# A convolution stem with its gradients on one core: Gelu in plain steps with its sums on ScalarE, three leaves by three products, stored sums of x, a shorter last product

## The chip, the cores and the metric

The kernel runs on one core of one Trainium2 chip. Its time is device microseconds of one execution, and the median of several executions stands for a kernel. All arrays are bf16, and products are added up in fp32 in PSUM. TensorE (PE) multiplies; VectorE (DVE) and ScalarE (ACT) work element by element; SyncE (SP) issues nearly all DMAs. "us" is microseconds.

## The reference

A one-dimensional convolution with 31 taps and stride 2 over B = 2 sequences of T = 16000 positions with D = 256 channels gives L = 7985 positions. Each channel of each sequence is then normalised over its positions, scaled and shifted, and passed through Gelu in its tanh form. The kernel also returns the gradients of x, w, gamma and beta for a given gradient of the output.

```python
h = jnp.einsum('blc,cd->bld', x[:, 0:s * L:s, :], w[0])
for i in range(1, K):
    h = h + jnp.einsum('blc,cd->bld', x[:, i:i + s * L:s, :], w[i])
mu = jnp.einsum('bld->bd', h)[:, None, :] / L
var = jnp.einsum('bld->bd', (h - mu) ** 2)[:, None, :] / L
h = (h - mu) / jnp.sqrt(var + 1e-5)
h = h * gn_gamma[None, None, :] + gn_beta[None, None, :]
return _gelu(h)
```

The outputs are Gelu's result and, from the vector-Jacobian product with grad_out, dx, dw, dgamma and dbeta.

## The kernel before

**Order.** The program first records every operation with `add`: its engine, what it reads and writes, and a function that issues it. Then `emit` issues the operations in the order that the table STEPS gives, as differences of positions in the record. Each engine works off its own instructions in that order and waits where operands are late. The order is thus written out by hand; the costs beside each `add` do not set it. SP's queue holds loads, stores and DMA transposes alike.

**Forward convolution (0 to about 385 us).** For each sequence b there are four chunks c of 2048 output positions (three full, one of 1841). A chunk is computed in three branches B_, A, C_, and a branch in three leaves B_, A, C_, since a convolution in two parts can be had from three products instead of four: the sums of inputs are made on DVE (`f_sums`, L492), the differences of weights too (`w_sub`, L473). A leaf is computed in one of two ways. `f_leaf` runs over all its taps: 64 matmuls of 256 columns. By three products it is split once more: `f_three_b` multiplies a difference of weights (WD) into one half of a PSUM buffer with 16 matmuls, ACT copies that half negated into the other (L550), and `f_three_ac` adds 32 more. A branch that is `split` does this for all three leaves; a `plain` one only for leaf B_. The set FV lists the branches that are split: nearly all of b = 0; for b = 1 the branches B_ and, in chunk 3, A and C_. The differences WD live in bytes that the Gelu of b = 0 uses later, so `f_again` computes four of them anew ahead of chunk 3 of b = 1. The evictions are at L574 (`keep`) and L596 on ACT, and the joins of leaves at L623 on DVE.

**Gelu.** Sequence 0's normalisation, Gelu and its derivative run during the forward convolution of sequence 1 (about 205 to 375 us), sequence 1's during the input gradient of sequence 0 (about 410 to 575 us): 8 units of 2048 elements per partition each, `gelu_unit`. A unit's steps: two ACT passes per half for y and its square (L860), a scalar_tensor_tensor on DVE (L862), sigmoid and another pass on ACT (L864, L866), a tensor_scalar (L868) and products on DVE (L872), and per half one accumulating copy on ACT (L885) and one tensor_tensor_reduce on DVE (L888) for the two sums that gamma and beta need. The units take turns with two sets of tiles (GT); for b = 0 set 1 lies at REG + 20480 and up. Two DMA transposes (L309) turn y of each unit for the output.

**Input gradient (about 390 to 803 us).** Stages G0 to G7, one per chunk and sequence, with matmuls of 512 columns at L1068.

**Weight gradient (803 to 1095 us).** Nine combinations n of a sum or difference of x with one of the gradient, stages W0 to W8, each with up to three products over both sequences. `x_tile` fetches the four tiles of x for the next combination: a raw block, a sum of two raw blocks (`x_raw` twice and `w_add`, L1322), or, for sequence 0, a stored sum that `x_pre` made during the forward convolution (xs_d). A combination begins with two adds into XSUM (L1322), sums of neighbouring rows (`pair_x`) and differences of the gradient (`leaf_d`, both L1312), and `pair_d` (L1418). PE's matmuls are at L1359 (`w_pairs`, `w_single`). The results are gathered by `w_done` (sums at L1365, the last one at L1387).

## Time and profile before

| | before |
|---|---|
| median of 3 runs | 1096.27 us (1095.95 to 1098.23) |
| the profiled execution, its own time | 1097.28 us |
| its span in the profile | 1095.2 us |
| PE busy, matmuls | 1080.6 us, 8123 recorded |
| PE weight loads | 8162 |
| DVE busy | 996.0 us |
| ACT busy | 608.9 us |
| mean granted clock of TensorE | 0.998 |

A matmul here always follows a weight load, so the number of weight loads, 8162, is the number of matmuls; a few records of matmuls are missing from the trace. "Busy" on PE is no more than having a matmul under way. In the profile's rows "a<-b" is what an instruction writes and reads, "xN" a count, and what stands after "<-" in brackets is what ended the idle time before.

### The profile page before, as it was taken

Reading aid. Unit: us, or ns where it says so; the run is one execution under the profiler, and the core shown is the slowest. Engines: PE = TensorE matmul, PEld = TensorE weight load, DVE = VectorE, ACT = ScalarE, POOL = GpSimd, SP = SyncE. Lnnn points to the kernel's source line nnn. Section 1 sums busy time; section 2 is a strip of 40 time slices with the busy share of each in tenths; the row PEclk is TensorE's granted clock in tenths of the full one; section 3 lists DMA queues with packets and bytes.
Section 4 is the critical chain, followed back from the end, with each engine's and each line's share of the span. In section 5 each row is a group of like instructions: output and inputs, shape, how many; then the busy total and the mean of one; then the engine's idle time right before and its main releaser. Section 6 shows DMA issues by size and latency. Waiting matters only on the chain.

```text
span 1095.2 us, 19717 instructions
## 1 busy us (share of the span) xinstructions
PE 1080.6 (99%) x8123; PEld 796.9 (73%) x8162; DVE 996.0 (91%) x1033; ACT 608.9 (56%) x855; POOL 9.8 (1%) x26
## 2 busy tenths in 40 slices
PE   8999999999999999999999999999999999999998
PEld 6888899988889984444444444444478888887887
DVE  6996777999999998999999998988799999999995
ACT  2244344789877569887966667675643223232332
POOL 0000000000000000000000000000000000000000
PEclk9999999999999999999999999999999999999999
DMA  9679999887979698998687999879898555897684
GB/s 246 122 190 241 270 263 260 237 172 185 205 170 219 195 311 267 254 268 249 169 270 218 296 301 363 243 246 327 271 332 226 200 162 173 273 355 237 198 231 137
DMA packets 346894, 261.48 MB, mean 239 GB/s; under 512 B 187702, under 2 KB 315572, under 8 KB 340916
## 3 DMA queue, kind: packets, MB, share of 16 engines
q1 hardware_dynamic: 346612, 260.22, 84.6%
q8 instruction: 64, 1.05, 0.4%
q14 instruction: 26, 0.21, 0.1%
q0 software_dynamic: 192, 0.00, 0.0%
HBM read 120.00 MB, written 94.86 MB: 196 GB/s over the span
## 4 chain that ended last, share of the span: by engine, by line
PE 86%; DVE 8%; DMA 2%; ACT 2%; issue 1%; SPq 0%; DVEq 0%; ACTq 0%
PE ps L521 35%; PE ps L1068 34%; PE ps L1359 16%; DVE arena L1322 3%; DVE arena L1312 3%; DVE arena L1365 1%; DVE arena L1418 1%; DMA arena<-d2d 1%; DMA arena<-in_x_dram 1%; DMA arena<-in_w_dram 1%; ACT arena L860 0%; SPq L303 0%; ACT arena L574 0%; DVE arena L492 0%; ACT ps L1095 0%
## 5 line engine op out<-in xcount | busy, mean ns | idle before, releaser
L1068 PE MATMUL ps<-arena 128*128 128x512 bf16 (+1 forms) x1834 | 397.5, 377 | 2.3 <-ACT ps L1095 0.3
L521 PE MATMUL ps<-arena 128*128 128x256 bf16 (+3 forms) x3684 | 393.4, 270 | 4.1 <-DMA arena<-in_x_dram 1.7
L521 PEld LDWEIGHTS <-arena 128*128 128x128 bf16 x3684 | 357.9, 98 | 40.4 <-DMA arena<-in_x_dram 2.5
L1068 PEld LDWEIGHTS <-arena 128*128 128x128 bf16 x1872 | 183.3, 98 | 216.2 <-issue 0.6
L574 ACT ACTIVATE arena<-ps 128x1024 bf16<-128x1024 f32 x189 | 191.6, 1021 | 238.8 <-PE ps L1359 115.4
L1359 PE MATMUL ps<-arena 128*128 128x256 bf16 x2592 | 285.1, 274 | 2.9 <-DVE arena L1312 2.9
L1359 PEld LDWEIGHTS <-arena 128*128 128x128 bf16 x2592 | 254.1, 98 | 34.0 <-DVE arena L1312 3.5
L492 DVE TENSOR_TENSOR arena<-arena 128x2080 bf16<-128x2080 bf16 (+8 forms) x133 | 163.1, 1252 | 11.9 <-PE ps L521 11.1
L1312 DVE TENSOR_TENSOR arena<-arena 128x4096 bf16<-128x4096 bf16 (+2 forms) x50 | 107.3, 2171 | 0.1
L872 DVE TENSOR_TENSOR arena<-arena 128x2048 bf16<-128x2048 bf16 (+1 forms) x80 | 95.5, 1197 | 4.7 <-ACT arena L864 2.1
L1031 DVE TENSOR_TENSOR arena<-arena 128x1032 bf16<-128x1032 bf16 (+6 forms) x111 | 85.6, 799 | 5.7 <-PE ps L1068 5.6
L1095 ACT ACTIVATE ps<-ps 128x512 f32<-128x512 f32 x108 | 62.9, 585 | 48.2 <-PE ps L1068 48.2
L1110 DVE TENSOR_TENSOR arena<-arena 128x1024 bf16<-128x1024 bf16 (+1 forms) x70 | 63.4, 915 | 13.5 <-ACT arena L574 13.1
L860 ACT ACTIVATE arena<-arena,stats 128x1024 bf16<-128x1024 bf16 (+1 forms) x64 | 74.6, 1209 | 1.2 <-DVE stats L806 0.8
L1322 DVE TENSOR_TENSOR arena<-arena 128x4096 bf16<-128x4096 bf16 x32 | 72.6, 2288 | 1.8 <-DMA arena<-in_x_dram 1.7
L1254 DVE TENSOR_TENSOR arena<-arena 128x1536 bf16<-128x1536 bf16 (+3 forms) x56 | 62.1, 1124 | 5.4 <-DMA d2d<-arena 4.3
L1431 ACT COPY ps<-ps 128x512 f32<-128x512 f32 x54 | 30.5, 570 | 64.8 <-PE ps L1359 64.8
L1418 DVE TENSOR_TENSOR arena<-arena 128x2048 bf16<-128x2048 bf16 x54 | 64.3, 1222 | 0.0
L550 ACT ACTIVATE ps<-ps 128x512 f32<-128x512 f32 x58 | 33.8, 583 | 53.8 <-PE ps L521 53.2
L623 DVE TENSOR_TENSOR arena<-arena 128x1024 bf16<-128x1024 bf16 (+3 forms) x52 | 43.4, 843 | 17.8 <-ACT arena L596 9.6
L473 DVE TENSOR_TENSOR arena<-arena 128x2048 bf16<-128x2048 bf16 (+1 forms) x48 | 51.4, 1087 | 7.0 <-DMA arena<-in_w_dram 2.9
L1365 DVE TENSOR_TENSOR arena<-arena 128x1024 bf16<-128x1024 bf16 x75 | 49.3, 690 | 8.3 <-ACT arena L574 8.0
(71 smaller groups left out, 462.8 us busy)
## 6 DMA issues: line engine op xcount, KB each, us to landing
arena<-in_x_dram SPq DMA_DIRECT2D x28, 1024.0 KB, 8.5
arena<-d2d SPq DMA_DIRECT2D x16, 1216.0 KB, 7.4
out_dram<-arena SPq DMA_DIRECT2D x35, 512.0 KB, 5.1
...
```

Of the source, the lines that this page charges most:

```text
L492: lambda p=p, q=q, r=r: nc.vector.tensor_tensor(out=p, in0=q, in1=r, op=ALU.add))
L521: yield nc.tensor.matmul(ps[:, dh, cs], lhsT=wt, rhs=mv, start=s0, stop=False, skip_group_check=True)
L574: lambda: nc.scalar.activation(out=out, in_=ps, func=ACT.Copy, scale=scale))
L860: lambda o=o, func=func, i=h[:, dh], sc=sc, bi=bi: SC.activation(out=o, in_=i, func=func, bias=bi, scale=sc))
L872: add("DVE", dve(8 * wd), [o], [a, b_], lambda: V.tensor_tensor(out=o, in0=a, in1=b_, op=op))
L1031: lambda: nc.vector.tensor_tensor(out=o, in0=a, in1=b, op=ALU.add))
L1068: yield nc.tensor.matmul(ps[:, e, 0:wide], lhsT=lt, rhs=mv, start=s0, stop=False, skip_group_check=True)
L1110: add("DVE", dve(o.free_size(), rate), [o], [a, b], lambda: nc.vector.tensor_tensor(out=o, in0=a, in1=b, op=op))
L1312: add("DVE", dve(o.free_size()), outs, ins, lambda: nc.vector.tensor_tensor(out=o, in0=a, in1=b, op=op), kind=kind + " weight_grad")
L1322: add("DVE", dve(4096), [o], [a, b], lambda: nc.vector.tensor_tensor(out=o, in0=a, in1=b, op=ALU.add))
L1359: yield nc.tensor.matmul(ps[:, s, c0:c1], lhsT=lt, rhs=mv, start=s0, stop=False, skip_group_check=True)
L1418: add("DVE", dve(2048), [d4], [d], lambda: nc.vector.tensor_tensor(out=d4, in0=fan(d[:, o0:o0 + 3 * s + 1:s, :], 1, (o1 - o0) * D), in1=fa ...
```

## The change

**Leaves.** In sequence 1's chunk 2, branch A is now split, and branch C_ is `mixed`: leaves B_ and C_ by three products, A over all its taps. The weight differences for sequence 1 are kept in a new place, WD1, at REG + 20480 and up, where Gelu's tile set 1 and its output tile lie; `f_again` makes three of them ahead of chunk 2's branch A and the fourth ahead of chunk 3's. Units 6 and 7 of sequence 0's Gelu use tile set 0.

**Gelu.** The scalar_tensor_tensor becomes a tensor_scalar and a product. The two tensor_tensor_reduce of a unit become one product of 2048 and two more accumulating copies on ACT.

**Sums of x.** Two more sums of blocks of x, both for sequence 1, are made during the forward convolution of sequence 1 (`x_late`: 8 times two loads of 256 KB, an add of 1024 and a store), and `x_tile` loads them for combinations 2 and 4 instead of two raw blocks and an add of 4096 each.

**Weight gradient.** Combination 6 writes its sums of x to XR instead of XSUM, and uses two places for pairs instead of three. The last product of all is computed for the one tap that is stored, with half the matmuls and half the add.

**Order.** STEPS is new throughout.

```diff
 STEPS = (
-    "0 2 10 -7 17 -16 25 -24 1 5 -4 1 -9 2 8 -7 10 1 1 1 15 1 1 1 5 -4 -17 18 4 -3 1 3 3 -27 26 3 -4 9 -4 1 -3 -26 30 3 -2 5 -1 -1 4 -37 42 -6 -33 44 -1 "
...
+    "2 4 6 -5 -7 22 -9 18 -28 8 -7 10 1 1 1 17 -2 1 4 -2 -17 22 -1 -1 3 -5 9 -26 24 1 -2 5 -1 -37 43 -44 42 -27 28 -2 4 -5 7 1 -2 4 -34 39 -6 10 -47 48 "
...
+    WD1 = {k: sb(REG + 20480 + 4096 * j, 2, 2, 2, D) for j, k in enumerate(((A, A), (A, C_), (C_, C_), (C_, A)))}
...
+    def x_late(k, s):
+        v = slice(2 * k, 2 * k + 2)
+        e, f = (TP[:, i].rearrange("p (n f) -> p n f", n=2) for i in range(2))
+        for t, k4 in ((e, 2), (f, 0 if s else 3)):
+            load(t, xblk(1)[:, v, k4, :], 262144, 1024)
+        add("DVE", dve(1024), [e], [e, f], lambda: nc.vector.tensor_tensor(out=e, in0=e, in1=f, op=ALU.add))
+        load(xs_d[s, 1, 0][:, v, :], e, 262144, 2048, "POOL")
...
-    def f_three_b(ps, br, lf, op, co, we):
+    def f_three_b(ps, br, lf, op, co, we, b=0):
+        wd = WD1[br, lf] if b and (br, lf) in WD1 else WD[br, lf]
...
-    FV = {(0, c, br) for c in range(NCK) for br in ORDER if c or br != B_} | {(1, c, B_) for c in range(NCK)} | {(1, 3, br) for br in (A, C_)}
+    FV = {(0, c, br) for c in range(NCK) for br in ORDER if c or br != B_} | {(1, c, B_) for c in range(NCK)} | {(1, 2, A), (1, 3, A), (1, 3, C_)}
...
+        def mixed(b, c, br, sums, co, we, wo):
+            ops, third, second = sums
+            x = free.pop(0)
+            u = slot(2)
...
+            keep(TX, flat2(ring[x]))
+            t = free.pop(0)
+            f_three_b(ring[t], br, C_, ops[C_], co, we, b)
+            v = slot(2)
+            third(C_, v)
+            f_join(TX, TX, RB[:, 1], ALU.add if br == A else ALU.subtract)
+            def last(lf):
+                if lf == A:
+                    f_leaf(ring[x], br, A, ops[A], co, we, wo, False)
+                    f_evac(b, c, br, A, ring[x], RB, ALU.add if br == A else ALU.subtract)
+                    free.append(x)
+                else:
+                    f_three_ac(ring[t], br, C_, v, co, we, wo)
+                    f_evac(b, c, br, C_, ring[t], fan(TX, 1, 0), ALU.subtract)
+                    free.append(t)
+            rest.extend([lambda: last(C_), lambda: last(A)])
...
                 for br in ORDER:
-                    if (b, c, br) == (1, 3, A) and (b, c, br) in FV:
-                        f_again()
+                    if (b, c, br) == (1, 2, A):
+                        f_again((A, A), (A, C_), (C_, C_))
+                    if (b, c, br) == (1, 3, A):
+                        f_again((C_, A))
                     if (b, c, br) == (0, 0, B_):
...
                     else:
-                        (split if (b, c, br) in FV else plain)(b, c, br, f_sums(xt, b, c, br, 12 * b + 3 * c + ORDER.index(br)), *f_width(c))
+                        (split if (b, c, br) in FV else mixed if (b, c, br) == (1, 2, C_) else plain)(b, c, br, f_sums(xt, b, c, br, 12 * b + 3 * c + ORDER.index(br)), *f_width(c))
                     if (b, c, br) == (1, 3, C_):
...
-    def f_again():
-        for br in (A, C_):
-            for lf in (A, C_):
-                v = W[br][:, lf]
-                w_sub(WD[br, lf], v[:, :, 1:4:2], v[:, :, 0:4:2])
+    def f_again(*keys):
+        for br, lf in keys:
+            v = W[br][:, lf]
+            w_sub(WD1[br, lf], v[:, :, 1:4:2], v[:, :, 0:4:2])
...
-                gelu_unit(b, c, e, (hs_[n % nset], ys_[n % nset], y2s[n % nscr], zs[n % nscr], ss_[n % nset]),
+                k = n % nset if b or n < 6 else 0
+                gelu_unit(b, c, e, (hs_[k], ys_[k], y2s[n % nscr], zs[n % nscr], ss_[k]),
                           gt.rearrange("p k d f -> p d k f")[:, :, :, off:off + HM], oo)
...
+        def tt(o, a, b_, op):
+            add("DVE", dve(8 * wd), [o], [a, b_], lambda: V.tensor_tensor(out=o, in0=a, in1=b_, op=op))
...
                     lambda o=o, func=func, i=h[:, dh], sc=sc, bi=bi: SC.activation(out=o, in_=i, func=func, bias=bi, scale=sc))
-        add("DVE", dve(8 * wd, 1), [z], [y2, y],
-            lambda: V.scalar_tensor_tensor(out=z, in0=y2, scalar=1.0 / GELU_A, in1=y, op0=ALU.add, op1=ALU.mult))
+        add("DVE", dve(8 * wd, 4), [z], [y2],
+            lambda: V.tensor_scalar(out=z, in0=y2, scalar1=1.0 / GELU_A, scalar2=None, op0=ALU.add))
+        tt(z, z, y, ALU.mult)
         add("ACT", act(8 * wd), [s], [z],
...
                                     op0=ALU.mult, op1=ALU.add))
-
-        def tt(o, a, b_, op):
-            add("DVE", dve(8 * wd), [o], [a, b_], lambda: V.tensor_tensor(out=o, in0=a, in1=b_, op=op))
         tt(y, y, s, ALU.mult)
...
         u = 2 * c + e
+        tt(z, s, h, ALU.mult)
         for dh in range(2):
-            sv, hh = s[:, dh], h[:, dh]
-            a0, a1 = esum[b][:, dh, 0, u:u + 1], esum[b][:, dh, 1, u:u + 1]
-            o = y2[:, dh]
-            add("ACT", act(4 * wd, 0.19), [o, a0], [sv],
-                lambda o=o, a0=a0, sv=sv: SC.activation(out=o, in_=sv, func=ACT.Copy, accum_out=a0))
-            o = z[:, dh]
-            add("DVE", dve(4 * wd, 1), [o, a1], [sv, hh],
-                lambda o=o, a1=a1, sv=sv, hh=hh: V.tensor_tensor_reduce(out=o, in0=sv, in1=hh, scale=1.0, scalar=0.0,
-                                                                        op0=ALU.mult, op1=ALU.add, accum_out=a1))
+            for i, o in ((0, y2[:, dh]), (1, z[:, dh])):
+                v, ac = (s[:, dh], z[:, dh])[i], esum[b][:, dh, i, u:u + 1]
+                add("ACT", act(4 * wd, 0.19), [o, ac], [v],
+                    lambda o=o, ac=ac, v=v: SC.activation(out=o, in_=v, func=ACT.Copy, accum_out=ac))
         if b == 0:
...
         else:
-            if (b, k3) in PRE and B_ in (i1, i2):
-                load(t, xs_d[2 if i1 == C_ else int(i2 == C_), b, k3][:], 1 << 20, 4096)
+            s = 2 if i1 == C_ else int(i2 == C_)
+            if (s, b, k3) in xs_d and B_ in (i1, i2):
+                load(t, xs_d[s, b, k3][:], 1 << 20, 4096)
...
             if (n, r3, h) == (8, 1, 1):
-                add("DVE", dve(1024, 1), [o], [ps, t], lambda: nc.vector.tensor_tensor(out=o, in0=flat2(ps), in1=t, op=ALU.add))
+                o_, i_, t_ = o[:, 512:], ps[:, 1], t[:, 512:]
+                add("DVE", dve(512, 1), [o_], [i_, t_], lambda: nc.vector.tensor_tensor(out=o_, in0=i_, in1=t_, op=ALU.add))
             else:
...
-    def w_single(ps, h, pd, xs):
-
-        for j in range(2):
+    def w_single(ps, h, pd, xs, js=(0, 1)):
+        for j in js:
             jobs = []
...
                         jobs.append((1 - j, s * D, s * D + D, xs[b][:, 2 * f + 1 - j, so * P:(so + 1) * P], pd[b][1][:, j, f, :], False))
-            w_mm(ps, jobs, [ps[:]], [xs[0], xs[1], pd[0][1][:, j], pd[1][1][:, j], ps[:]])
+            o = ps[:] if len(js) == 2 else ps[:, 1]
+            w_mm(ps, jobs, [o], [xs[0], xs[1], pd[0][1][:, j], pd[1][1][:, j], o])
...
         def place(n):
-            ks = (0, 1) if n in (0, 3, 5) else (0, 1, 2)
+            ks = (0, 1) if n in (0, 3, 5, 6) else (0, 1, 2)
             turn_[0] += 1
...
             pm = place(n)
+            xsum = XR if n == 6 else XSUM
             for b in range(NB):
-                w_add(XSUM[b], xt[b, 0], xt[b, 1])
-            pair_x(pm, XSUM)
+                w_add(xsum[b], xt[b, 0], xt[b, 1])
+            pair_x(pm, xsum)
             pa, pc = place(n), place(n)
...
                 for h in range(2):
-                    w_single(G[h], h, pd, lx[i3])
+                    w_single(G[h], h, pd, lx[i3], (0, 1) if (n, r3, h) != (8, 1, 1) else (0,))
                     w_done(n, G[h], h, r3, PM[h] if pd else None)
...
+    XLATE = {(1, 0, A): ((0, 2),), (1, 0, C_): ((1, 2),), (1, 1, B_): ((2, 2),), (1, 1, A): ((3, 2), (0, 0)), (1, 1, C_): ((1, 0),), (1, 2, B_): ((2, 0), (3, 0))}
...
                 x_pre(k)
+            plan.hold = -1
+        for k, s in XLATE.get((b, c, br), ()):
+            plan.hold = plan.npe
+            x_late(k, s)
             plan.hold = -1
```

The order on ACT in the first 40 us, from the last cast of the transposed input on. ps0 to ps3 are the four PSUM buffers; L550 and L562 are the negated copies, L574 and L586 the evictions. Before:

```order
L431 CAST arena_110<-ps2_116 128x4x4x16 [waits PE_49]
L574 ACTIVATE arena_110<-ps0_114 128x1024 [waits PE_49]
L574 ACTIVATE arena_110<-ps1_115 128x1024 [waits DVE_49,PE_49]
L550 ACTIVATE ps3_117<-ps3_117 128x512 [waits PE_49,Activation_49]
L574 ACTIVATE arena_110<-ps3_117 128x1024 [waits PE_49,Activation_49]
L550 ACTIVATE ps2_116<-ps2_116 128x512 [waits PE_49]
L550 ACTIVATE ps3_117<-ps3_117 128x512 [waits PE_49,Activation_49]
```

In the change:

```order
L442 CAST arena_112<-ps2_118 128x4x4x16 [waits PE_49]
L562 ACTIVATE ps3_119<-ps3_119 128x512 [waits PE_49,Activation_49]
L586 ACTIVATE arena_112<-ps3_119 128x1024 [waits PE_49,Activation_49]
L586 ACTIVATE arena_112<-ps1_117 128x1024 [waits DVE_49]
L562 ACTIVATE ps2_118<-ps2_118 128x512 [waits PE_49]
L586 ACTIVATE arena_112<-ps0_116 128x1024
```

The first negated copy and the eviction of its buffer ps3 now stand ahead of the evictions of the two plain leaves in ps0 and ps1.

DVE's order in sequence 1's chunk 2, where `f_again` now begins (L484 is `w_sub`, L899 Gelu's products of unit 5 and later, L503 the sums of inputs, L635 the joins). In the change:

```order
L899 TENSOR_TENSOR arena<-arena 128x2048 [waits DMAHW6_49,DMAHW3_49,Activation_49]
L899 TENSOR_TENSOR arena<-arena 128x2048 [waits DVE_49,Activation_49]
L503 TENSOR_TENSOR arena<-arena 128x8x258 [waits PE_49]
L635 TENSOR_TENSOR arena<-arena 128x4x256 [waits Activation_49]
L899 TENSOR_TENSOR arena<-arena 128x2048 [waits DVE_49]
L503 TENSOR_TENSOR arena<-arena 128x2x4x262 [waits DVE_49]
L899 TENSOR_TENSOR arena<-arena 128x2048 [waits DVE_49]
L899 TENSOR_TENSOR arena<-arena 128x2048 [waits DMAHW4_49,DMAHW0_49,DVE_49]
L484 TENSOR_TENSOR arena<-arena 128x2048 [waits DMAHW7_49,DMAHW0_49]
L503 TENSOR_TENSOR arena<-arena 128x2x4x262 [waits PE_49]
```

The first difference waits for two DMA queues, which carry the transposes of unit 5's y (L309) out of the bytes that it overwrites; behind it stand sums for the next branch. Before, the first four differences stood in chunk 3, behind the last unit's sums.

DVE's order where combination 5 of the weight gradient begins. L1322 and L1363 are the adds of x, L1312 and L1353 with 4608 elements the leaf differences and with 4096 or 2048 the pair sums, L1365 and L1407 sums of results, L1418 and L1461 `pair_d`. The piece begins with the first add into XSUM and ends with the first pair sum that PE reads in combination 5. Before:

```order
L1322 TENSOR_TENSOR arena<-arena 128x4096 [waits DMAHW6_49,DMAHW0_49,PE_49]
L1365 TENSOR_TENSOR arena<-arena 128x1024 [waits Activation_49]
L1365 TENSOR_TENSOR arena<-arena 128x1024
L1312 TENSOR_TENSOR arena<-arena 128x4608 [waits DMAHW5_49,DMAHW6_49,DVE_49,PE_49]
L1322 TENSOR_TENSOR arena<-arena 128x4096 [waits DMAHW7_49]
L1418 TENSOR_TENSOR arena<-arena 128x2048 [waits DVE_49]
L1312 TENSOR_TENSOR arena<-arena 128x4096 [waits DVE_49]
```

In the change:

```order
L1363 TENSOR_TENSOR arena<-arena 128x4096 [waits DMAHW7_49,DMAHW4_49,PE_49]
L1353 TENSOR_TENSOR arena<-arena 128x4608 [waits DMAHW4_49,DMAHW5_49,DVE_49,PE_49]
L1353 TENSOR_TENSOR arena<-arena 128x4608 [waits DVE_49,PE_49]
L1363 TENSOR_TENSOR arena<-arena 128x4096 [waits DMAHW6_49]
L1353 TENSOR_TENSOR arena<-arena 128x4096 [waits DVE_49]
```

One leaf difference stood ahead of that pair sum, and both do now.

DVE's order from combination 5's last add of an x tile (the first row) to combination 6's pair sums. Before:

```order
L1322 TENSOR_TENSOR arena<-arena 128x4096 [waits DMAHW4_49,DMAHW1_49]
L1365 TENSOR_TENSOR arena<-arena 128x1024 [waits Activation_49]
L1365 TENSOR_TENSOR arena<-arena 128x1024
L1365 TENSOR_TENSOR arena<-arena 128x1024 [waits DVE_49]
L1418 TENSOR_TENSOR arena<-arena 128x2048 [waits PE_49] x2
L1365 TENSOR_TENSOR arena<-arena 128x1024 [waits Activation_49]
L1365 TENSOR_TENSOR arena<-arena 128x1024 [waits DVE_49] x2
L1322 TENSOR_TENSOR arena<-arena 128x4096 [waits DMAHW6_49,DMAHW5_49]
L1365 TENSOR_TENSOR arena<-arena 128x1024 [waits DVE_49]
L1322 TENSOR_TENSOR arena<-arena 128x4096
L1312 TENSOR_TENSOR arena<-arena 128x2048 [waits PE_49]
```

In the change:

```order
L1363 TENSOR_TENSOR arena<-arena 128x4096 [waits DMAHW7_49,DMAHW2_49]
L1363 TENSOR_TENSOR arena<-arena 128x4096 [waits DVE_49]
L1353 TENSOR_TENSOR arena<-arena 128x4096 [waits PE_49]
L1407 TENSOR_TENSOR arena<-arena 128x1024 [waits Activation_49]
L1407 TENSOR_TENSOR arena<-arena 128x1024
L1407 TENSOR_TENSOR arena<-arena 128x1024 [waits DVE_49]
L1461 TENSOR_TENSOR arena<-arena 128x2048 [waits PE_49] x2
L1407 TENSOR_TENSOR arena<-arena 128x1024 [waits DVE_49]
L1407 TENSOR_TENSOR arena<-arena 128x1024 [waits Activation_49]
L1353 TENSOR_TENSOR arena<-arena 128x2048 [waits DMAHW4_49,PE_49]
L1407 TENSOR_TENSOR arena<-arena 128x1024 [waits DVE_49]
L1363 TENSOR_TENSOR arena<-arena 128x4096 [waits DMAHW3_49]
```

Combination 6's two adds are the rows L1322 with 4096 elements toward the end, before; in the change they are the second row, right behind the last x tile, and the last row. Before, eight instructions stood between that x tile and the first of the two adds.

19 lines of the change are left out of this document (13 added, 6 removed), and 152 rows, old and new, of the table STEPS.

## The prediction

> **What bounds the kernel now.** I read the page first, then the windows of 25 us, then what TensorE waited for, and last the timeline around the two places where it stood still.
>
> ```profile
> span 1095.2 us, 19717 instructions
> PE 1080.6 (99%) x8123; PEld 796.9 (73%) x8162; DVE 996.0 (91%) x1033; ACT 608.9 (56%) x855; POOL 9.8 (1%) x26
> ```
>
> A PE that is busy 99% of the span says little by itself; the windows say whether it runs at its own pitch. Columns: PE, weight loads, DVE, ACT, POOL busy with their counts, granted clock, DMA share, GB/s.
>
> ```profile
> 225.00:250.00 25.00, 25.00 (x230) 22.28 (x229) 24.03 (x24) 19.41 (x29) 0.00 (x0) 1.00 0.71 160
> ...
> 975.00:1000.00 25.00, 22.29 (x191) 19.11 (x189) 25.00 (x20) 6.23 (x8) 0.00 (x0) 0.93 0.94 328
> 1000.00:1025.00 25.00, 25.00 (x232) 22.39 (x230) 24.96 (x23) 6.61 (x9) 0.00 (x0) 1.00 0.67 223
> ...
> PE ps L1359 <- DVE arena L1312: 2.9, 2, 2.7
> PE ps L1068 <- ACT ps L1095: 0.3, 1, 0.3
> ```
>
> From 50 us on, a stretch of the two convolutions or of the weight gradient holds 230 or 231 matmuls of 256 columns: 25.00/231 = 0.108 us each, with no room between. So PE's own work sets the time, and a matmul that goes is worth 0.108 us. One window falls out: 975 to 1000 has 191 instead of 231, and there DVE is busy 25.00 of 25.00. The last two rows, from the list of what waited for what (total, times, longest), are all that PE lost to DVE in the weight gradient and to ACT in the input gradient.
>
> **The matmuls that go.** A leaf of the second batch element's chunk 2 costs 4x2x2x2x2 = 64 matmuls when computed plainly and 16+32 = 48 by three products. Two leaves lose 16 each; the leaf C,C has no tap 31 and falls from 56 to 44. The last product of the weight gradient is half as long: 32 to 16. That is 44+16 = 60, and the instruction list of PE is shorter by 120, a weight load and a matmul each. 60 x 0.108 = **6.5 us**, all on the path. The price is three more evictions on ACT and some DVE work, below.
>
> **The waits in the first 40 us.**
>
> ```profile
> 25.79 1.02 ACT L574 ACTIVATE arena<-ps 128x1024 bf16<-128x1024 f32 x1 [5.99 <-PE ps L521]
> 27.61 0.58 ACT L550 ACTIVATE ps<-ps 128x512 f32<-128x512 f32 x1 [0.79 <-PE ps L521]
> 28.24 5.42 PE L521 MATMUL ps<-arena 128*128 128x256 bf16 x48 [0.73 <-ACT ps L550]
> ...
> 33.70 0.58 ACT L550 ACTIVATE ps<-ps 128x512 f32<-128x512 f32 x1 [0.67 <-PE ps L521]
> 34.33 1.92 PE L521 MATMUL ps<-arena 128*128 128x256 bf16 x16 [0.67 <-DVE arena L473]
> ```
>
> Twice PE ends a difference product, ACT copies it negated (0.58), and PE, which has nothing else, waits 0.73 and 0.67. In the new order eight matmuls of a plain leaf (0.87) stand in the first place and a difference product of 16 (1.73) in the second. Both are longer than the wait that they cover: **-1.4 us**. From both sides: -1.7 by the gaps between weight loads, 0 if the operands are late instead.
>
> **The stop at 992 us.**
>
> ```profile
> 890.37 4.49 DVE L1322 TENSOR_TENSOR arena<-arena 128x4096 bf16<-128x4096 bf16 x2 [1.66 <-DMA arena<-in_x_dram]
> ...
> 929.23 0.77 PEld L1359 LDWEIGHTS <-arena 128*128 128x128 bf16 x8 [0.49 <-DVE arena L1312]
> ...
> 989.31 2.29 DVE L1322 TENSOR_TENSOR arena<-arena 128x4096 bf16<-128x4096 bf16 x1
> 991.51 7.03 DVE L1312 TENSOR_TENSOR arena<-arena 128x2048 bf16<-128x2048 bf16 x4
> 995.00 6.25 PE L1359 MATMUL ps<-arena 128*128 128x256 bf16 x41 [2.71 <-DVE arena L1312]
> 995.00 6.08 PEld L1359 LDWEIGHTS <-arena 128*128 128x128 bf16 x42 [2.99 <-DVE arena L1312]
> ...
> 995.00:998.20 3.20, 3.20 (x16) 2.27 (x17) 3.20 (x2) 0.00 (x0) 0.00 (x0) 0.50 1.04 311
> ```
>
> DVE works without a pause through the weight gradient except for 1.66 us at 888.7, where a raw block of x is late, and by combination 6 it is behind: its pair sums end at 994.9 while PE has been free since 992.1. PE loses 2.9 us. Then the granted clock is 0.50 for 3.2 us: 16 matmuls where 3.20/0.108 = 29.6 would fit, another 13.6 x 0.108 = 1.5. The Trainium skill ("TensorE: Matmul & The Clock Gate", What's actually happening) gives half rate after an idle window of about 3.4 us; here 2.7 to 3.0 were enough, and the measurement decides. By the Trainium skill's figure the 1.5 would not be this stop's, nothing of it would come back, and the time would be 1.5 above the forecast.
>
> The change takes two adds from DVE's queue ahead of this point:
>
> ```profile
> L1322 DVE TENSOR_TENSOR arena<-arena 128x4096 bf16<-128x4096 bf16 x32 | 72.6, 2288 | 1.8 <-DMA arena<-in_x_dram 1.7
> ...
> 797.20 2.28 DVE L1322 TENSOR_TENSOR arena<-arena 128x4096 bf16<-128x4096 bf16 x1
> 799.40 0.68 DVE L1110 TENSOR_TENSOR arena<-arena 128x1024 bf16<-128x1024 bf16 x1
> ...
> 806.82 7.22 DVE L1312 TENSOR_TENSOR arena<-arena 128x4096 bf16<-128x4096 bf16 x3
> ...
> 803.10 9.12 PE L1359 MATMUL ps<-arena 128*128 128x256 bf16 x82
> ```
>
> Each add holds DVE for 2.20 (797.20 to 799.40), so 4.4 us go, more than the 2.9 that DVE was late. The starts give the room: PE begins the weight gradient at 803.1, DVE its share at 806.8, 3.7 behind. From there DVE's queue to combination 6's pair sums is 188.1 long with the 1.66 in it (806.8 to 994.9) and PE's to the same point 189.0 (803.1 to 992.1). For the new order I add up what stands in both queues, at 2.47, 2.20, 1.13 and 0.61 us for 4608, 4096, 2048 and 1024 elements and 0.1088 a matmul (the 7.22 of the third row are 2.28 and two leaf differences of 2.47; the row names only the first one's form). Up to combination 5's first pair sum that is 150.9 for DVE and 156.7 for PE: 5.8, less the late start of 4.0 that the sums give before, leaves 1.8 to spare. Combination 6 keeps 1.4, and its first x add stands right behind combination 5's last one, because it writes another buffer and no longer waits for PE. The next to be late is therefore combination 5, which has both leaf differences (2.47 each) ahead of its first pair sum. The change also removes one of the two raw blocks around 888, so the 1.66 may go or stay; if it stays the 1.8 is 0.1. I take the stop as gone: **-4.4**, and the 0.49 of combination 4 with it: **-0.4**. Bounds: 0 if DVE stays behind, -4.9.
>
> **The end.**
>
> ```profile
> 1091.13 1.22 DVE L1387 TENSOR_TENSOR arena<-ps,arena 128x1024 bf16<-128x1024 f32 x1 [1.70 <-PE ps L1359]
> ```
>
> Half the elements. The trace has no PSUM read of 512 by this line; between no gain and half, nearer half: **-0.5**.
>
> **What is added, and what hides it.**
>
> ```profile
> L862 DVE SCALAR_TENSOR_TENSOR arena<-arena 128x2048 bf16<-128x2048 bf16 x12 | 27.5, 2288 | 2.8 <-ACT arena L860 2.7
> L868 DVE TENSOR_SCALAR arena<-arena 128x2048 bf16<-128x2048 bf16 x12 | 8.3, 690 | 0.2
> L872 DVE TENSOR_TENSOR arena<-arena 128x2048 bf16<-128x2048 bf16 x60 | 73.1, 1222 | 4.2 <-ACT arena L864 2.1 <-ACT arena L866 1.4
> L888 DVE CUSTOM_DVE_ANT_0 arena<-arena 128x1024 bf16<-128x1024 bf16 x24 | 28.6, 1220 | 0.1
> L885 ACT ACTIVATE arena<-arena 128x1024 bf16<-128x1024 bf16 x24 | 25.1, 1048 | 8.1 <-DVE arena L872 8.1
> L388 DVE TENSOR_TENSOR arena<-arena 128x1024 bf16<-128x1024 bf16 x24 | 16.2, 685 | 1.9 <-DMA arena<-in_x_dram 1.9
> L492 DVE TENSOR_TENSOR arena<-arena 128x2064 bf16<-128x2064 bf16 x39 | 48.2, 1236 | 6.9 <-PE ps L521 6.5 <-issue 0.3
> L623 DVE TENSOR_TENSOR arena<-arena 128x2048 bf16<-128x2048 bf16 x18 | 21.9, 1219 | 7.9 <-ACT arena L574 7.9
> ...
> 200.00:395.00 195.00, 195.00 (x1813) 176.96 (x1811) 182.84 (x207) 148.75 (x217) 3.46 (x7) 1.00 0.87 206
> 400.00:575.00 175.00, 173.84 (x824) 82.17 (x840) 166.44 (x205) 141.66 (x170) 1.44 (x4) 1.00 0.87 245
> ```
>
> Gelu, per unit of 2048: 2288 becomes 690+1222, and two reductions of 1220 become one product of 1222: DVE loses 1.6 us, 16 units some 25 us, half in each stretch. ACT gains two accumulating copies a unit: 32 x 1.05 = 33 us, again half and half. In 200:395 DVE gets back eight adds of 685 (5.5), three thirds of 1236 (3.7) and 1.9 of joins, so it falls from 182.8 to about 181. ACT rises to 148.8+16.7+3x0.58 = 167 of 195 (86%), and in 400:575 to 158 of 175 (90%). All of this lies beside PE while no queue is full. DVE, at 95% in 400:575, was nearer to full than ACT will be, and PE lost 0.3 us to ACT there in all (above).
>
> The eight early sums also put 24 DMAs on SP's queue, 6 MB, ahead of the transposes of x for chunks 1 and 2; DMA share was 0.87.
>
> The new wait is for weights. Their differences now go to where unit 5 of the Gelu batch kept its tiles, so on DVE the first difference waits for two transposes of y out of the same bytes, and behind it on DVE stand the sums of the next branch, which PE needs.
>
> ```profile
> L309 SPq DMA_TRANSPOSE arena<-arena x16: 1231/1277/2188, 226.3 to 360.6; - x16
> DMA to landing us min/median/max: 3.2/4.8/7.3
> ...
> 359.30 3.48 SPq L309 DMA_TRANSPOSE arena<-arena  x2
> ...
> 374.31 2.36 DVE L473 TENSOR_TENSOR arena<-arena 128x2048 bf16<-128x2048 bf16 x2
> ```
>
> Between the product that completes y and that difference stand seven DVE instructions: five of some 1.23, one of 1.25 and one of 0.69 make 8.1, about 7.5 as they overlap. The transposes need 1.3 for the first issue and 4.8 (3.2 to 7.3) to land: 6.1, so 1.4 to spare, or 1.1 late. Before, the same differences stood in chunk 3: the transposes were issued from 359.3 to 362.8 and the first difference ran at 374.3, so at 7.3 to land there were 4 us to spare at the worst. I add **+1.0** for this and for ACT's fuller queue together, from 0 to 6.
>
> **The sum.** -6.5 -1.4 -4.4 -0.4 -0.5 +1.0 = -12.2: the span of 1095.2 becomes 1083.0. The profiled execution took 1097.28, 2.1 over its span, and the median of the runs shown is 1096.27, 1.0 below it; so 1085.1 for a profile and **1084.1** for the median.
>
> **Rivals.**
> 1. *DVE stays behind*: the stop at combination 6 moves to combination 5, whose slack was put at 0.1 to 1.8. For it: DVE still has next to no idle time in the weight gradient. Against: 4.4 us less to do. Time: 1084.1+4.4 = 1088.5; chance 0.12.
> 2. *The reused bytes are late*: transposes slowed by the 24 new DMAs land 3 to 5 us later than above, and PE stands still in chunk 2 for 2 to 4 us, then at half clock for 1.5. For it: a margin of 1.4. Against: transposes of 7.3 at most among 36 that share the queue. Time: about 1088.5; chance 0.10.
> 3. *ACT becomes the bound*, the slower case: at 86 to 90% of a queue that runs in order, an accumulating copy whose product is late holds back the evictions that PE waits for, at 200 to 395 and 400 to 575. ACT's idle time there, 46 and 33 us, is mostly spent waiting for PE and DVE. If only two fifths of the 33 us find a place, 20 us lie on the path: 1104; it decides from 12 us on. Against: 33 us is under half of that idle time. Chance 0.05.
> 4. *The DVE relief was never on the path and the orders of the first 40 us bring nothing*: only the matmuls and the end count, 1096.3-7.0 = 1089.3; chance 0.05.
>
> **How the numbers follow.** The forecast has 0.68, its own range 1082 to 1086. Two runs of this kernel differ by about 0.2% (2.2 us), so faster means under 1094.1. All but rival 3 are faster: 0.93 with the mixtures between; 0.02 for the same, where several small losses add to 10 us; 0.05 slower. The range must take in the costs' bounds below (every wait gone, 0.3 more at the start and none added: 1082.3) and rivals 1, 2 and 4 above, mixed with a further 3 us: 1081 to 1092.
>
> **What would show it.** Right: the window around combination 6 holds 230 matmuls at clock 1.00; no wait of PE for ACT or DVE before 40 us; PE's count down by 60; ACT near 167 and 158 in the two stretches with PE full. Wrong: a PE wait for a DVE subtraction near 325 us (rival 2), for the pair sums at the start of combination 5 (rival 1), or many waits of some tenths for ACT evictions between 200 and 575 (rival 3).

## The result

Six runs of the changed kernel have a median of 1088.91 us (1087.65 to 1090.35), beside 1097.25 for six runs of the kernel before: a ratio of 0.9926, interval 0.9913 to 0.9938. The change gains 8.3 us, where 12.2 were forecast; 1088.9 lies inside the range of 1081 to 1092, which was drawn to take in the rivals, but 4.8 above the forecast and outside the forecast's own range of 1082 to 1086. The profiled execution took 1087.65 us with a span of 1085.7, so 2.6 of the 4.8 are in its profile; the other 2.3 are the step from the profile to the median.

The page of the changed kernel, and its windows (columns as before: PE, weight loads, DVE, ACT, POOL, granted clock, DMA share, GB/s):

```profile
span 1085.7 us, 19692 instructions
PE 1074.9 (99%) x8102; PEld 790.3 (73%) x8102; DVE 979.5 (90%) x1012; ACT 638.2 (59%) x922; POOL 9.8 (1%) x26
```

```profile
200.00:395.00 195.00, 195.00 (x1818) 177.58 (x1816) 182.33 (x209) 167.40 (x253) 3.42 (x7) 1.00 0.95 239
400.00:575.00 175.00, 174.72 (x822) 80.31 (x820) 157.90 (x191) 155.60 (x196) 1.44 (x4) 1.00 0.86 248
950.00:975.00 25.00, 23.40 (x216) 20.73 (x213) 23.61 (x16) 6.92 (x9) 0.00 (x0) 1.00 0.85 291
975.00:1000.00 25.00, 24.90 (x229) 22.08 (x227) 25.00 (x22) 6.82 (x10) 0.00 (x0) 1.00 0.75 249
```

Everything that the trace lists of PE's waits, in total, times and longest:

```profile
PE ps L532 <- DMA arena<-in_x_dram: 1.6, 1, 1.6
PE ps L1401 <- DVE arena L1353: 1.6, 1, 1.6
PE ps L436 <- DVE zt L368: 1.3, 1, 1.3
PE ps L532 <- DVE arena L503: 0.7, 2, 0.4
PE ps L532 <- DVE arena L484: 0.5, 1, 0.5
PE ps L1109 <- ACT ps L1136: 0.3, 1, 0.3
```

Three things are seen at once. PE has 60 weight loads fewer and is full in both stretches of Gelu, with ACT at 167.4 and 155.6 us. The window 975 to 1000, which held the stop at combination 6, has 229 matmuls instead of 191. But 950 to 975 has 216: there is a new stop, at the start of combination 5.

For the account, all weight loads of both traces are sorted by the stage that their matmuls belong to. F0 to F7 are the chunks of the forward convolution, G0 to G7 those of the input gradient, W0 to W8 the combinations, which are counted from 0. A stage lasts from its weight loads' starts to the next ones'; stages not listed differ by less than 0.1 us.

```
stage           before (loads)   change (loads)   difference, us
F0              59.33 (494)      58.32 (494)      -1.01
F6              53.48 (488)      51.72 (472)      -1.76
F7              55.84 (548)      52.77 (520)      -3.07
G0              59.04 (276)      59.37 (276)      +0.33
W3              31.92 (288)      31.44 (288)      -0.48
W4              31.35 (288)      33.31 (288)      +1.96
W5              34.42 (288)      31.71 (288)      -2.71
W6              32.95 (288)      31.35 (288)      -1.60
W8              31.33 (288)      29.58 (272)      -1.75
last load to the end of the span
                 4.51             4.97            +0.46
```

The sum is -9.6; the spans differ by 9.5.

### The profile page after: what moved, and what is told of

Read it like the earlier page. It is cut to its first block, busy times and chain, and to the rows that moved or that the text cites. A ratio compares the mean times of both kernels' runs of the same rounds, so it can differ in the third digit from the quotient of the medians.

```text
span 1085.7 us, 19692 instructions
## 1 busy us (share of the span) xinstructions
PE 1074.9 (99%) x8102; PEld 790.3 (73%) x8102; DVE 979.5 (90%) x1012; ACT 638.2 (59%) x922; POOL 9.8 (1%) x26
## 4 chain that ended last, share of the span: by engine, by line
PE 93%; DVE 4%; SPq 1%; DMA 1%; ACT 0%; issue 0%; DVEq 0%; ACTq 0%
PE ps L1109 36%; PE ps L532 34%; PE ps L1401 22%; SPq L305 1%; DVE arena L1363 1%; DVE arena L1353 1%; DMA arena<-in_x_dram 1%; DVE arena L1461 1%; DVE arena L1407 1%; DMA arena<-in_w_dram 0%; DVE arena L484 0%; ACT arena L914 0%; ACT L912 0%; ACT ps L1136 0%; ACT arena L586 0%
## 5 line engine op out<-in xcount | busy, mean ns | idle before, releaser
L532 PE MATMUL ps<-arena 128*128 128x256 bf16 (+3 forms) x3640 | 388.7, 270 | 2.9 <-DMA arena<-in_x_dram 1.6
L586 ACT ACTIVATE arena<-ps 128x1024 bf16<-128x1024 f32 x191 | 192.5, 1023 | 195.7 <-PE ps L1401 82.4
L1401 PE MATMUL ps<-arena 128*128 128x256 bf16 x2576 | 281.7, 273 | 1.7 <-DVE arena L1353 1.6
L503 DVE TENSOR_TENSOR arena<-arena 128x2064 bf16<-128x2064 bf16 (+6 forms) x136 | 166.1, 1250 | 21.0 <-PE ps L532 15.8
L899 DVE TENSOR_TENSOR arena<-arena 128x2048 bf16<-128x2048 bf16 (+1 forms) x112 | 133.5, 1197 | 6.6 <-ACT arena L912 2.5
L1353 DVE TENSOR_TENSOR arena<-arena 128x4096 bf16<-128x4096 bf16 (+2 forms) x50 | 107.3, 2169 | 0.9 <-PE ps L1401 0.7
L562 ACT ACTIVATE ps<-ps 128x512 f32<-128x512 f32 x61 | 35.4, 586 | 74.3 <-PE ps L532 74.1
L1363 DVE TENSOR_TENSOR arena<-arena 128x4096 bf16<-128x4096 bf16 x30 | 67.8, 2286 | 2.2 <-DMA arena<-in_x_dram 1.3
L930 ACT ACTIVATE arena<-arena 128x1024 bf16<-128x1024 bf16 (+1 forms) x64 | 65.6, 1028 | 6.5 <-DVE arena L899 6.3
L1461 DVE TENSOR_TENSOR arena<-arena 128x2048 bf16<-128x2048 bf16 x54 | 64.5, 1220 | 1.9 <-PE ps L1109 1.8
L484 DVE TENSOR_TENSOR arena<-arena 128x2048 bf16<-128x2048 bf16 (+1 forms) x48 | 51.5, 1085 | 4.8 <-DMA vl<-arena 2.3
L1407 DVE TENSOR_TENSOR arena<-arena 128x1024 bf16<-128x1024 bf16 x75 | 49.0, 686 | 6.6 <-ACT arena L586 6.3
```

What stands on the lines that cost most here:

```text
L503: lambda p=p, q=q, r=r: nc.vector.tensor_tensor(out=p, in0=q, in1=r, op=ALU.add))
L532: yield nc.tensor.matmul(ps[:, dh, cs], lhsT=wt, rhs=mv, start=s0, stop=False, skip_group_check=True)
L586: lambda: nc.scalar.activation(out=out, in_=ps, func=ACT.Copy, scale=scale))
L899: add("DVE", dve(8 * wd), [o], [a, b_], lambda: V.tensor_tensor(out=o, in0=a, in1=b_, op=op))
L930: lambda o=o, ac=ac, v=v: SC.activation(out=o, in_=v, func=ACT.Copy, accum_out=ac))
L1353: add("DVE", dve(o.free_size()), outs, ins, lambda: nc.vector.tensor_tensor(out=o, in0=a, in1=b, op=op), kind=kind + " weight_grad")
```

## Experiments on the new stop

This is DVE, then SyncE, then PE in the changed kernel around it (start, duration, engine, line, operation; in brackets the idle time ahead and what ended it; SPq is SyncE issuing DMAs, here five in a row):

```profile
945.04 2.55 DVE L1353 TENSOR_TENSOR arena<-arena 128x4608 bf16<-128x4608 bf16 x1
948.10 2.56 DVE L1353 TENSOR_TENSOR arena<-arena 128x4608 bf16<-128x4608 bf16 x1 [0.51 <-PE ps L1401]
951.98 2.29 DVE L1363 TENSOR_TENSOR arena<-arena 128x4096 bf16<-128x4096 bf16 x1 [1.32 <-DMA arena<-in_x_dram]
954.30 2.29 DVE L1353 TENSOR_TENSOR arena<-arena 128x4096 bf16<-128x4096 bf16 x1
```

```profile
944.60 11.02 SPq L305 DMA_DIRECT2D arena<-in_x_dram  x5
```

```profile
956.65 124.46 PE L1401 MATMUL ps<-arena 128*128 128x256 bf16 x1136 [1.60 <-DVE arena L1353]
```

DVE is not behind here: it waits 1.32 us for a raw block of x. SyncE issues that block's load only at 944.60, because it goes into a buffer whose last reader, a `w_single` of combination 4, ends on PE at 944.6. Load 7.4, add 2.3 and pair sum 2.3 make 956.6, and PE's last weight load before the stop was at 954.7. Before, the block for the same tile went into the other of the two buffers XR. Raw blocks take turns there (`xrc`). The two new stored sums are loaded during combinations 2 and 4, one for a tile of combination 3 and one for a tile of combination 5. Each takes one raw block out of the turns, and the first of them shifts the turn of the block in question by one. XR[0] lies over the sums of x that `w_pairs` reads early in a combination, XR[1] over the differences that `w_single` reads to its end. A theory, then: the transfer sets the stop. The rival is the prediction's own: DVE has too much ahead of the pair sum.

**The other buffer.** One turn is skipped ahead of combination 5's tiles:

```diff
             if n < 8:
+                if n == 4:
+                    xrc[0] += 1
                 for k in KEYS:
                     xt[k] = x_tile(n + 1, *k)
```

> The changed kernel, but the raw block of x that completes combination 5's last tile but one is loaded into the other of the two buffers for raw blocks; the rotation of the later ones follows. Theory (the block's transfer sets combination 5's start: its buffer is freed by the last product of combination 4, then load, add of 4096, pair sum): the load starts some 6 us earlier, DVE no longer waits 1.32 for it, and the stop of 1.98 us between weight loads at combination 5 falls to 0.5 or less; span and time 1.4 us shorter. Rival (DVE has too much work ahead of the pair sum): the stop stays between 1.5 and 2.0, the time within 0.3 us.

```profile
938.43 18.01 SPq L305 DMA_DIRECT2D arena<-in_x_dram  x5
```

```profile
948.92 2.56 DVE L1353 TENSOR_TENSOR arena<-arena 128x4608 bf16<-128x4608 bf16 x1 [0.52 <-PE ps L1401]
951.39 2.28 DVE L1363 TENSOR_TENSOR arena<-arena 128x4096 bf16<-128x4096 bf16 x1
953.71 2.29 DVE L1353 TENSOR_TENSOR arena<-arena 128x4096 bf16<-128x4096 bf16 x1
```

The load goes out 6.2 us earlier, DVE no longer waits for it, and the gap between weight loads (from the start of one to the start of the next, 0.11 where nothing waits) falls from 1.98 to 0.57. The median is 1086.49 us (four runs, 1086.12 to 1087.01), 0.9901 of before, interval 0.9888 to 0.9915: some 2.4 below the change's 1088.91. The theory holds. That the median falls by more than the 1.4 that the profiles differ by at this place fits with the transfer's length, which varies from one execution to the next, and with the clock, which halves behind a longer stop here (both below); how much each makes is not shown.

**DVE's order.** The leaf difference that starts at 948.10 is moved behind the pair sum; only the table of the order changes. In words:

```diff
-leaf difference of 4608
 pair sum's x tile: add of 4096        (waits for the raw block)
 pair sum of 4096
+leaf difference of 4608
```

> The changed kernel with combination 5's second leaf difference (2.47 us) moved on DVE from ahead of the first pair sum to behind it. Theory (the transfer sets it): DVE waits for the raw block 2 to 4 us instead of 1.32, the pair sum ends where it did, and the stop stays between 1.8 and 2.1 us; time unchanged. Rival (DVE's queue sets it): the stop is gone and the time 1.9 us shorter.

```profile
945.58 2.55 DVE L1353 TENSOR_TENSOR arena<-arena 128x4608 bf16<-128x4608 bf16 x1
953.57 2.29 DVE L1363 TENSOR_TENSOR arena<-arena 128x4096 bf16<-128x4096 bf16 x1 [5.44 <-DMA arena<-in_x_dram]
955.89 4.76 DVE L1353 TENSOR_TENSOR arena<-arena 128x4096 bf16<-128x4096 bf16 x2
```

```profile
960.71 3.60 PE L1401 MATMUL ps<-arena 128*128 128x256 bf16 x16 [5.11 <-DVE arena L1353]
```

With 2.5 us less ahead of it, DVE waits 5.44 us for the block instead of 1.32; the add is not sooner for it, in this execution even 1.6 us later. That is the theory's side. The stop, though, was expected unchanged and grew to 5.5, because the products that open combination 5 read this leaf difference too, and it now ends at 960.6. The median is 1093.15 (1091.94 to 1094.22), 0.9961 of before. The expectation had missed that the moved instruction was itself on the path.

**Two adds put back.** On top of the other buffer, combinations 2 and 4 make their second sum of x twice:

```diff
             for b in range(NB):
                 w_add(xsum[b], xt[b, 0], xt[b, 1])
+            if n in (2, 4):
+                w_add(xsum[1], xt[1, 0], xt[1, 1])
```

> The kernel with the raw block in the other buffer, and with the second sum of x of combinations 2 and 4 made twice on DVE: 2 x 2.2 us put back there, no transfer changed, nothing left out. Theory (DVE has next to nothing to spare by combinations 5 and 6, so the two adds that the change removed were on the path): stops of 2.5 to 4.5 us in all at combinations 5 and 6, with half clock for 3 us behind the longer one if it is over 2.5; time 1089 to 1092. Rival (the two adds were covered, the raw block alone made the stops): time within 0.5 us of 1086.5.

```profile
862.63 63.08 PE L1401 MATMUL ps<-arena 128*128 128x256 bf16 x576 [0.67 <-DVE arena L1353]
926.56 31.61 PE L1401 MATMUL ps<-arena 128*128 128x256 bf16 x288 [0.85 <-DVE arena L1353]
959.27 0.94 PE L1401 MATMUL ps<-arena 128*128 128x256 bf16 x7 [1.09 <-DVE arena L1353]
```

PE now stops for pair sums at the start of combinations 2, 4 and 5, with gaps of 1.04, 1.23 and 1.47 us between weight loads, and the median is 1089.16 (1089.0 to 1090.08), 2.7 above the same kernel without the adds. The size was as expected, the places were earlier. So DVE has next to nothing to spare from combination 2 on, and work of this size put back on it is on the path. The adds put back stand at the start of a combination, where those that the change took away stood toward the end of one, so this is the price of 4.4 us more on DVE and not of the very same adds.

**DVE's order again, with the block early.** From these three the next step was to let DVE add the tile first, then make the leaf difference, the pair sum, and only then the second leaf difference; and to issue two late stores sooner, of which more below. DVE's order, in words:

```diff
 add of 4096 into XSUM
+x tile: add of 4096
-leaf difference of 4608 (not needed yet)
 leaf difference of 4608
-x tile: add of 4096
 pair sum of 4096
+leaf difference of 4608 (not needed yet)
```

> The kernel with the raw block in the other buffer, and besides: at combination 5 DVE adds the x tile first, then makes the leaf difference that the first products need, their pair sum, and only then the second leaf difference; the two late stores of the output are issued 8 us earlier; the last product's store is the last in SyncE's queue. Theory (the transfer and the order of DVE set the stop; the end is set by the bytes that still move): the stop of 0.57 at combination 5 falls below 0.2, from the last weight load to the end 4.5 instead of 4.95, time 1085.5 us (1084.9 to 1086.3). Rival (the end is a fixed latency after the last store): the end stays at 4.9 and the time at 1086.

```profile
978.46 8.89 PE L1401 MATMUL ps<-arena 128*128 128x256 bf16 x80 [0.42 <-ACT arena L586]
988.15 2.03 PE L1401 MATMUL ps<-arena 128*128 128x256 bf16 x17 [0.79 <-DVE arena L1353]
```

The 0.57 at combination 5 is gone as expected, but gaps of 0.69 within it, behind an eviction, and of 1.17 at combination 6 have come: PE arrives earlier at sums that DVE has not made sooner. The median is 1087.41 (1087.01 to 1088.08), above the 1085.5 that was expected and not below the other buffer alone. With DVE as full as it is here, this order only moved the places where PE waits.

## Experiments on the end

The last product is half as long and its DVE add takes 0.69 instead of 1.22, as forecast. Yet from the last weight load to the end it takes 0.46 longer. The last rows of DVE and SyncE:

```profile
1080.50 0.69 DVE L1407 TENSOR_TENSOR arena<-arena 128x1024 bf16<-128x1024 bf16 x1 [2.85 <-ACT arena L586]
1081.14 0.69 DVE L1430 TENSOR_TENSOR arena<-ps,arena 128x512 bf16<-128x512 f32 x1
```

```profile
1075.02 7.75 SPq L305 DMA_DIRECT2D out_dram<-arena  x7
```

The product before last ends only 1.7 us before the last one, where it was 3.5, so that its two stores and the last one are all issued after 1081.2, the last at 1082.3 to 1082.8. Before, the last store was issued by itself, 0.40 after the last add.

**Another queue.** One of the two stores goes through ScalarE's queue:

```diff
+                if i == 30:
+                    add("ACT", 0.4, [out_], [in_], lambda out_=out_, in_=in_: nc.scalar.dma_start(out=out_, in_=in_), dma=0.5)
+                else:
+                    load(out_, in_, 131072, 512, "POOL", slack=60.0)
```

> The changed kernel with one store of the product before last (tap 30) issued by ScalarE's queue instead of SyncE's. Theory (the last product is now so short that the stores of the one before it stand in SyncE's queue with the last store): from the last matmul to the end of the span 4.1 us instead of 4.6. Rival (the landing of the last bytes sets the end whatever queue issues them): 4.5 to 4.7. No difference in the time that could be told from noise either way.

The last issue is 0.40 behind the last add again instead of 0.93, but from it to the end of the span it is 3.46 us instead of 2.93: the end is where it was, 4.97 after the last weight load. The rival holds: it is not the queue. The median, 1090.13 (1088.04 to 1090.67), is not to be told from the change's either. The windows show what is still under way. The first three rows are the changed kernel's last stretch, the other four the kernel before's, from a like distance of the end:

```profile
1081.00:1082.00 1.00, 0.11 (x1) 0.00 (x0) 0.84 (x2) 0.00 (x0) 0.00 (x0) 1.00 0.98 281
1082.00:1083.00 1.00, 0.00 (x0) 0.00 (x0) 0.00 (x0) 0.00 (x0) 0.00 (x0) 1.00 0.82 229
1083.00:1084.00 1.00, 0.00 (x0) 0.00 (x0) 0.00 (x0) 0.00 (x0) 0.00 (x0) 0.69 0.78 220
```

```profile
1090.50:1091.50 1.00, 0.59 (x6) 0.29 (x3) 0.37 (x1) 0.00 (x0) 0.00 (x0) 1.00 0.84 227
1091.50:1092.50 1.00, 0.00 (x0) 0.00 (x0) 0.86 (x1) 0.00 (x0) 0.00 (x0) 1.00 0.03 8
1092.50:1093.50 1.00, 0.00 (x0) 0.00 (x0) 0.00 (x0) 0.00 (x0) 0.00 (x0) 1.00 0.20 58
1093.50:1094.50 1.00, 0.00 (x0) 0.00 (x0) 0.00 (x0) 0.00 (x0) 0.00 (x0) 0.69 0.26 73
```

PE's last matmul ends at 1081.1 in the change and at 1091.1 before. The DMA engines still move bytes at shares of 0.98, 0.82 and 0.78 in the three microseconds after PE's end; before, from 0.4 us behind PE's end on, they were at 0.03 to 0.26. A theory, then: PE ended sooner, the bytes of the last results and of two stores of the output did not.

**The late stores earlier.** Two stores of the output (`out0_late`, 512 and 408 KB) are ready long before, and are issued at 1074.4 and 1075.0. The other buffer, with these two put 8 us earlier in the order and nothing else moved:

> The kernel with the raw block in the other buffer, and the two late stores of the output issued 8 us earlier, nothing else moved: DVE's order at combination 5 as in the change. Theory: stop of 0.57 at combination 5 and 0.3 at combination 6 as with the block alone, from the last weight load to the end 4.55 instead of 4.95, time 0.4 us below that of the block alone, 1086.1 (1085.5 to 1086.8). Rival (what the end wins is lost again to scatter at the start): no difference from 1086.5 that the interval tells.

From the last weight load to the end it is 4.65 us instead of 4.94 (4.55 in the kernel with DVE's order). The median is 1086.29 (1086.06 to 1086.97), ratio 0.9901, interval 0.9885 to 0.9918. So the late stores make 0.3 of the 0.46, as read from one profile of each kernel; the time cannot tell it, and 0.14 above the 4.51 of before is left unexplained. This is the lowest median, 2.6 us below the change and 10.9 below before, but it is not to be told from the other buffer alone (1086.49).

## Experiments on Gelu and ScalarE

**Gelu as before.** The changed kernel with the old steps of a unit, in words:

```diff
-        tensor_scalar(z, y2, add), tt(z, z, y, mult)
+        scalar_tensor_tensor(z, y2, y)
-        tt(z, s, h, mult), 4 accumulating copies on ACT
+        2 accumulating copies on ACT, 2 tensor_tensor_reduce on DVE
```

> The changed kernel with the steps of Gelu as before (scalar_tensor_tensor, two tensor_tensor_reduce, two accumulating copies a unit), the rest as in the change. Theory (the relief of DVE in the forward convolution is what makes room for the three leaves and the early sums): DVE would need 182.3 + 12.8 = 195 of 195 us from 200 to 395, so PE stops there for 2 to 10 us in all, and the time is 1091 to 1099. Rival (nothing of it was on PE's path): no stop of PE there, time within 1 us of the change's 1089.

```profile
200.00:395.00 195.00, 192.68 (x1784) 173.98 (x1783) 189.44 (x217) 149.16 (x217) 3.40 (x7) 1.00 0.92 229
400.00:575.00 175.00, 173.06 (x805) 80.22 (x821) 166.30 (x201) 141.28 (x168) 1.44 (x4) 1.00 0.88 247
```

The median is 1095.31 (1094.37 to 1096.62), 0.9984 of before, interval 0.9975 to 0.9993. By stages F6 is 2.6 longer than in the change, F7 0.7, G0 1.1 and G2 1.3: 5.6 us in all for which PE waits for weight differences and sums on DVE. By the median 6.4 of the 8.3 us are lost again without the new steps of Gelu. The profile, whose span is 8.7 above the change's, also has 2.5 more in W4 and W5: the stop at combination 5 is 3.13 there, with half clock behind it, and the run doesn't show whether Gelu has a part in that. The profile before has no wait of PE in these stretches that they could remove; what they do is pay for the leaves and the early sums.

**The added copies twice.** The 32 copies that the change adds to ACT are each made a second time:

```diff
                 add("ACT", act(4 * wd, 0.19), [o, ac], [v],
                     lambda o=o, ac=ac, v=v: SC.activation(out=o, in_=v, func=ACT.Copy, accum_out=ac))
+                if i == 1:
+                    add("ACT", act(4 * wd, 0.19), [o, ac], [v],
+                        lambda o=o, ac=ac, v=v: SC.activation(out=o, in_=v, func=ACT.Copy, accum_out=ac))
```

> The changed kernel with the two accumulating copies that the change adds in each unit of Gelu made twice: 32 x 1.05 us more on ACT, half from 200 to 395 and half from 400 to 575, where ACT then needs 184 of 195 and 172 of 175 us. Nothing is left out. Theory (ACT's work lies beside PE until the queue is full): no loss of PE from 200 to 395, at most 3 us from 400 to 575; time 1088 to 1092. Rival (a queue in order holds back evictions long before it is full): 5 us or more, 1094 and up.

```profile
200.00:395.00 195.00, 188.62 (x1735) 169.01 (x1733) 172.16 (x192) 180.82 (x276) 3.40 (x7) 1.00 0.87 220
400.00:575.00 175.00, 165.34 (x782) 78.19 (x795) 145.90 (x179) 165.86 (x222) 1.44 (x4) 0.99 0.83 238
```

```profile
DVE arena L910 <- ACT arena L934: 24.5, 11, 4.0
PE ps L1113 <- ACT ps L1140: 5.4, 6, 1.4
PE ps L533 <- ACT arena L587: 3.9, 2, 2.0
PE ps L1113 <- ACT ps L587: 3.2, 2, 2.0
```

The median is 1109.52 (1108.2 to 1112.07), 20.6 above the change, and my expectation was wrong by far: the first 33 us on ACT cost PE at most the 0.33 of G0 in the change's first profile, the second 33 cost 20.6. ACT is busy for 93 and 95% there. DVE's products wait 24.5 us for the copies (L934) that still read the tiles, where they wait 4.1 in the change, and PE waits for evictions behind them. The cover that the prediction counted on was there, and nearly used up. Each second copy stands right behind the first one in an order that was written for one; whether ACT's fullness or this place makes the 20.6 is not separated.

## The same kernels once more

The changed kernel again, with five runs:

> The changed kernel once more, on the same chip. Theory (its times vary by what the raw block's transfer takes: a stop of 2 us leaves the clock, a longer one halves it for 3 us): times in two groups, about 1087.5 to 1088.3 and 1089.5 to 1090.5, and the profile shows either a stop of about 2.0 at clock 1.00 or one of 2.5 and more with the clock at 0.5 behind it. Rival (plain scatter): one group.

The times are 1088.60, 1088.62, 1089.48, 1090.05 and 1090.97 (median 1089.48, ratio 0.9926): a spread, not two groups. The profiled one took 1090.05, with a stop of 1.99 at combination 5 and the clock at 1.00 behind it, and 1.4 more in F6, 0.5 in F3 and 0.5 in F0 than the first profile. Of F6's part the trace says:

```profile
PEld L532 <- DVE arena L484: 0.8, 1, 0.8
PE ps L532 <- ACT arena L930: 0.5, 1, 0.5
```

This is DVE's weight difference (L484) of `f_again`, and a wait that the trace puts down to an accumulating copy on ACT. The late bytes were not the cause: DVE had work up to the difference. The other place that varies is the raw block: in the kernel with another queue for one store, which is the change at this point, DVE waited 2.24 us for it, PE 2.90, and the clock halved:

```profile
953.15 2.29 DVE L1363 TENSOR_TENSOR arena<-arena 128x4096 bf16<-128x4096 bf16 x1 [2.24 <-DMA arena<-in_x_dram]
...
957.80:961.00 3.20, 3.17 (x16) 2.29 (x17) 3.20 (x3) 0.00 (x0) 0.00 (x0) 0.52 1.01 331
```

That execution took 1090.01. So the two groups fall, and that the raw block makes part of the scatter stands.

The kernel before again:

> The kernel before once more, for a second profile of its first 55 us and of combinations 5 and 6. Theory (the first stage varies by what the first loads take, apart from the two waits for ACT): its first 494 matmuls take 58.8 to 59.8 us (59.33 in the profile before, 58.3 to 59.2 in those of the changed order), with waits of 0.9 to 1.0 at 27 and 33 us again, and the stop of 3.1 at combination 6 with half clock behind it is there again. Rival (the stop of the profile before was an accident): it is under 1.5.

Its first 494 matmuls take 59.41 us, with gaps of 1.00 and 0.81 at 27 and 33 us, and the stop at combination 6 is 3.09 again. The rival falls. But behind the stop the clock stayed at 1.00 this time (its rows stand in the last section), W6 is 1.60 shorter for it, and the execution, at 1095.72, was 1.56 below the first profile.

## Why the prediction was right, and where it was not

The direction and most of the terms came out; the size did not, and that it missed by no more has a part of luck: 0.7 of the 1.0 added for the reused bytes and ACT wasn't needed and made up for some of what combination 5 and the end cost.

| term | forecast | in the profiles |
|---|---|---|
| 60 matmuls fewer (F6, F7, W8) | -6.5 | -6.6 |
| order of the first 40 us (F0) | -1.4 | -1.0; -0.7 over ten profiles |
| stop at combination 6, with the clock (W5, W6) | -4.4 | -4.3 |
| late block at combination 4 (W3) | -0.4 | -0.5 |
| stop at combination 5 (W4) | 0 | +2.0 |
| the end | -0.5 | +0.5 |
| reused bytes and ACT | +1.0 | 0.0 (F5 to F7), +0.3 (G0) |

*The matmuls* came out to the tenth.

*The first 40 us.* Both waits for ACT are gone. Two others have come at 19 and 25 us, for DVE's weight differences (gaps of up to 1.3 and of 0.75 to 0.95), since PE reaches them sooner. F0 takes 58.67 us on average over the ten profiles with this order (58.29 to 59.16), and 59.33 and 59.41 in the two of before. So half of the gain came. What took the other half is what the prediction gave for its lower bound of 0, operands that are late instead.

*Combination 6.* The stop is gone, and the size was right with the clock in it. That DVE's shorter queue made it fits: putting 4.4 us back on DVE brings gaps of 3.7 us in all, where there is one of 0.57 without. They come at combinations 2, 4 and 5, though, and no run takes away the other buffer and the new order that combination 6 has in the change, so the shares of the two are open.

*Combination 5* is the step that failed. Its slack was put at 0.1 to 1.8 by adding up the durations of DVE's instructions. The pair sum hung on a transfer instead, whose start is set by when PE leaves a buffer, and the shift in the turns of two buffers made that 6 us later. The prediction had counted a raw block that goes and had not asked where the remaining ones land. Even with the block early the slack is -0.5, not 1.8. In that kernel, DVE's instructions from its first leaf difference of 4608 to this pair sum take 151.9 instead of the 150.9 that the prediction added up (the same counts; an add of 4096 takes 2.23 there and not 2.20), and two waits ahead of the pair sum were not in the sum:

```profile
DVE arena L1363 <- DMA out_dram<-arena: 1.0, 1, 1.0
DVE arena L1353 <- PE ps L1401: 0.5, 1, 0.5
```

Rival 1 named the place and the wrong cause; it was given 0.12 at 1088.5, and the time is 1088.9.

*The end.* The add's 0.5 came as forecast (1.22 to 0.69). What followed it was costed at nothing: the stores of the product before, now 1.7 us closer, and two late stores of the output.

*Reused bytes and ACT.* In the change's profile the difference in chunk 2 does not make PE wait; in the second profile F6 lost 1.4, within the 0 to 6 that was given. ACT came out at 167.4 and 155.6, forecast 167 and 158. Rival 3's mechanism is real, from the next 33 us on.

*The median.* It was taken 1.0 below the profile, as with the three runs of before that were known. Over six runs that profile stands at the median (1097.28 beside 1097.25), and the change's stands 1.3 below its own. The executions differ by the raw block, by the first loads, and by whether the clock halves behind a stop. Of the last the mean granted clock on record gives a count. A window of 3.41 us at half clock takes 1.7 us, 0.16% of the time, and the profiles with such a window ahead of PE's end have a mean of 0.998 or less, those without one 0.999 or 1.000. Of the change's 11 runs 7 have 0.998 or less, of the 32 of the kernel before whose clock is on record 30, and of the four with the block in the other buffer none.

What stays open is the 0.33 in G0, where the trace names only "issue" for a gap at 399.0, and what else than the clock makes one execution longer than another.
